# The logits' PSUM banks in one pool with the others, and an issue order written for it, in an attention and token-MLP block

## The chip, the core and the metric

The kernel runs on one core of a Trainium2 chip. The metric is the device time of one execution in microseconds (us); what is compared is the median of several executions.

## What is computed

One transformer block with conditioning, in bfloat16, for S = 2048 tokens of width D = 512:

```
sa, ca, ga, sb, cb, gb = (silu(c) @ w_mod) in six pieces
h = layernorm(x) * (1 + ca) + sa
# attention: 32 heads of 16, each query sees 8 keys, 2 positions apart, none before the start
x = x + ga * (local_attention(h @ wqkv) @ wo)
h = layernorm(x) * (1 + cb) + sb
# token MLP: mixes along S, F = 1792
u = gelu(einsum('bsd,sf->bdf', layernorm(h), w1) + b1)
x = x + gb * transpose(einsum('bdf,fs->bds', u, w2) + b2)
```

## The kernel before

The 2048 tokens are 16 tiles of 128. `SIZES = (2, 4, 4, 4, 2)` puts them into five chunks, and `build_chunk` (L634) records for each chunk the work of the attention: layer norm and its transposition, `qkv` products and their evacuations (`ev`), the products of query and key on DVE (`qk`), the sums over a head's 16 values as products with a 0/1 matrix on PE (`red`), which give the **logits**, then their maximum on DVE (`max`, L790), its subtraction by a product on PE (`sub`, L797), the exponential on ACT (`exp`, L800), the sum of the exponentials (`esum`), the softmax weights (`smB` on DVE). DMAs bring these weights into another layout (`a2`, four per chunk, into the tile `a2sb`) and the values too (`vd`, into a ring of five tiles `vD`); DVE multiplies the two (`pv`, four per chunk), PE sums (`pvacc`), ACT evacuates (`oev`). Then come the output projection (`wo`, one per token tile, L860), the residual sum (`x1`), the statistics of the second layer norm (`ln2q`, `rstd2`, `nb`, `n2`), its affine part on DVE (`aff`, two tiles per instruction, two passes), and the third layer norm (`ln3s` statistics, `rstd3`, `nb3`, `h3`). The token MLP's first product sums over tokens: `mlp1_{sweep}_{ft}_{tile}` (L927 on) adds the token tiles `h3`, as they get ready, for 14 blocks `ft` of 128 hidden values, and is parked in SBUF between sweeps (`park`, `padd`). `gelu`, the second product `mlp2_{tile}`, `fin` on DVE and the store `st_out` of each token tile end the kernel.

PSUM has eight banks of 512 float32 per partition. Six are single tiles `psS` (L313), a pool `ps` whose slots hold `qkv`, `esum`, `pvacc`, `wo` and MLP results; the other two are one tile `psL` (L314), which holds the logits of one chunk from the first `red` to `exp`. Chunks 1 to 3 use both of its banks, chunks 0 and 4 one.

The instruction order of every engine is written by hand in the string `ORDER` (L192 to 250). Each entry is an operation's name, with flags: `a`, `d`, `p` (ACT, DVE, POOL) or `s` (SP) choose the engine; on PE `q` splits each 128 x 128 product into four of 32 columns, one per column group of the array, and `n` leaves out a `wo`'s product that adds the residual (then `x1` adds it) or an `inj`. `fill:n` is n units of 128 columns of products that nobody reads. `schedule()` (L86) reads the string and gives each operation that needs a slot the free one that was freed longest ago. All engines issue through one wrapper, so every row of the profile has line L143; rows are told apart by their tiles. SP issues nearly all DMAs, in the string's order, and waits where one is not ready.

Of the kernel before, what the change touches and what calls it, by code (L numbers as in the profile page):

```python
# [8 lines left out]
ALU = mybir.AluOpType  # L9
# [4 lines left out]
P = 128  # L14
# [28 lines left out]
class _Graph:  # L43
# [42 lines left out]
    def schedule(self):  # L86
# [4 lines left out]
        for pos, token in enumerate(ORDER.split()):  # L91
# [22 lines left out]
            if o.alloc is not None:  # L114
                p = o.alloc.pool
                o.alloc.i = min((freed[p][k], k) for k in range(self.pools[p]) if held[p][k] is None)[1]
                held[p][o.alloc.i] = o.alloc
            if o.frees is not None:
                o.frees.left -= 1
                if o.frees.left == 0:  # L120
                    held[o.frees.pool][o.frees.i] = None
                    freed[o.frees.pool][o.frees.i] = pos
# [85 lines left out]
qk2_0 woq_s smB1 qk2_3 qkv2_01:q qkv2_12:q qkv2_02:q ev2_11:a ev2_01:a a2_1_1:a ev2_12:a ev2_02:a qk2_1 qk2_2 wo1:q  # L208
x1_1:a wo0:q x1_0:a ln2q1 xt10 xt12 red2_0 qkv2_23:q qkv3_22:q qkv3_12:q vd1_0 st_row1 vd1_2 ev2_23:a ln2q0 rstd2_0
nb1_4 nb2_0 qkv2_21:q ev2_21:a red2_1 a2_1_2:s a2_1_0:s a2_1_3:s vd1_1 ld_row1 vd1_3 n1_14:p pv1_2 qkv3_13:q red2_2  # L210
red2_3 max2 qkv2_22:q n1_15:a ev3_13:a n2_1:a ev3_12:a ev2_22:a n2_0:a halo_v2:p qkv2_20:q sub2:q ev2_20:a exp2
pvacc1_2 qkv3_10:q halo_v3:a oev1_2:a ev3_10:a qkv3_02:q qkv3_20:q pv1_1 qkv3_01:q pvacc1_1 esum2:q ev3_02:a ev3_20:a
ev3_22:a aff0 pv1_0 qkv3_03:q qkv3_00:q pvacc1_0 pv1_3 oev1_1:a ev3_01:a rcp2 halo_k3:a smB2 ln3s0 qkv3_11:q oev1_0:a
pvacc1_3 ev3_11:a oev1_3:a qkv3_23:q fill:1:q wo5:q wo3:q qk3_2 qk3_1 ld_w1_0_0 ld_w1_0_512 vd2_3 xt14 vd2_2 vd2_1
a2_2_1:s a2_2_0:s a2_2_2:s vd2_0 a2_2_3:s wo4:q ln3s1 ev3_03:a ev3_00:a qk3_0 x1_3:a x1_4:a qk3_3 ln2q3 ln2q4 x1_5:a
ev3_23:a qkv4_22:q qkv3_21:q ev3_21:a wo2:q red3_0 x1_2:a qkv4_20:q fill:2:q red3_1 qkv4_00:q red3_2 ev4_22:a ln2q5
ln2q2 ev4_20:a rstd2_2 pv2_0 rstd2_4 red3_3 pvacc2_0 oev2_0:a pv2_3 qkv4_12:q ev4_12:a qkv4_02:q nb2_2 ev4_02:a n2_2:a
max3 sub3:q pvacc2_3 exp3 esum3:q oev2_3:a rstd3_0 pv2_2 nb2_4 pvacc2_2 qkv4_10:q rcp3 n2_5:a oev2_2:a n2_4:a pv2_1
pvacc2_1 fill:4:q oev2_1:a wo6:q wo7:q wo8:q wo9:q ev4_00:a smB3 n2_3:p vd3_3 ld_w1_0_896 vd3_1 vd3_0 a2_3_2:s a2_3_3:s
a2_3_0:s a2_3_1:s vd3_2 ld_w2_1 aff2 nb3_0 aff4 h3_1:p h3_0:p halo_v4:p ln3s3:a ln3s2:d ln3s4:d ln3v3 ln3v2 ln3v4  # L220
ln3s5:a ln3v5 pv3_1 x1_8:a x1_7:a x1_6:a rstd3_2 ev4_10:a h3_3 h3_2 mlp1_0_1_0 mlp1_0_2_0 mlp1_0_5_0:q mlp1_0_3_0:q
pvacc3_1 rstd3_4 nb3_4 x1_9:a pv3_2 pv3_3 pv3_0 h3_4:a h3_5:a oev3_1:a mlp1_0_2_2:q mlp1_0_1_2:q mlp1_0_0_0:q
mlp1_0_0_2:q mlp1_0_3_2:q mlp1_0_0_4:q mlp1_0_5_2:q mlp1_0_5_4:q mlp1_0_3_4:q mlp1_0_1_4:q pvacc3_2 mlp1_0_2_4:q ln2q9
ln2q6 park0_0:a park0_1:a ln2q7 park0_2:a oev3_2:a qk4_0 qk4_2 mlp1_0_4_0:q mlp1_0_4_2:q pvacc3_3 mlp1_0_6_0:q ln2q8
oev3_3:a mlp1_0_6_2:q pvacc3_0 mlp1_0_6_4:q mlp1_0_4_4:q oev3_0:a mlp1_0_7_0:q wo13:qn red4_0 rstd2_6 nb2_6 park0_3:a
qk4_1 x1_13:d n2_9:a n2_6:a park0_4:a wo12:q n2_8:p ld_w1_0_1152 ld_w1_0_1408 vd4_1 ld_w2_3 vd4_2 vd4_0 vd4_3 n2_7:d
# [15 lines left out]
padd2_1 gelu1 gelu4 mlp1_2_3_11 mlp1_2_3_14 mlp1_2_2_14 mlp1_2_6_11 padd2_3 padd2_2 gelu2 padd2_6 gelu6 gelu3
mlp1_1_12_10 mlp1_2_5_11 mlp1_2_5_14 mlp1_1_11_10 padd2_5 padd1_11 gelu5 gelu9 padd1_12 mlp1_1_13_10 gelu12 gelu11
mlp2_0_0 padd1_13 gelu13 ld_w2_4 ld_w2_2 ld_w2_5 mlp2_0_0b ld_w2_7 ld_w2_9 ld_w2_11 ld_w2_13 mlp2_2_0 mlp2_6_0
mlp2_0_0c mlp2_3_0 mlp2_8_0 mlp2_4_0 fin0_0 st_out0_0 fin4_0 fin2_0 st_out2_0 fin6_0 st_out4_0 fpre gsc mlp2_9_0 fin3_0
fin8_0 st_out8_0 st_out6_0 mlp2_5_0 mlp2_1_0 fin1_0 mlp2_14_0 mlp2_10_0 st_out1_0 st_out3_0 fin5_0 ld_w2_15 fin10_0
# [7 lines left out]
def kernel(  # L254
# [34 lines left out]
    G = _Graph(dict(ps=6, big=NBIG, vd=NVD))  # L289
# [344 lines left out]
    def build_chunk(ch):  # L634
# [125 lines left out]

        for dlo in range(4):
# [316 lines left out]
```

## Time and profile before

| what | us |
|---|---|
| three runs | 198.40, 198.61, 198.69 (median 198.61) |
| the profiled execution | 198.75 |
| its span, from the first instruction to the last | 197.03 |
| busy in it: PE, DVE, ACT, POOL | 185.8, 157.3, 127.1, 22.8 |
| mean granted TensorE clock | 0.997 |

Rows of the timeline begin with the start and the length in us, then the engine, the line, the operation, what it writes <- what it reads, its shape, and how many instructions the row holds; behind it in brackets is the idle time before it and what ended that. 128\*128 and 128\*32 stand for the part of the array that a product uses. A product's end is modelled, so rows of PE overlap a little, and starts are the better guide.

### The profile page before, as it was taken

What the parts mean: (1) busy time and instruction counts of PE and PEld (TensorE: products, weight loads), DVE (VectorE), ACT (ScalarE), POOL (GpSimd) and SP (SyncE); (2) the same over time, 40 slices, a digit from 0 to 9 for tenths busy, and PEclk for the clock granted to TensorE, in tenths of its full rate; (3) what the DMA queues carried; (4) which work ended last, traced back from release to release, by engine and by line L of the source; (5) the groups of instructions that cost most, each with busy time, mean ns of one, the idle gap of its engine ahead of it and who ended that gap; (6) DMA issues with size and microseconds to landing.
All of it is one profiled execution on the core that took longest, in us unless ns stands there. A gap on an engine that the chain in (4) does not pass through costs nothing.

```text
span 197.0 us, 5568 instructions
## 1 busy us (share of the span) xinstructions
PE 185.8 (94%) x2331; PEld 99.5 (50%) x2343; DVE 157.3 (80%) x222; ACT 127.1 (64%) x304; POOL 22.8 (12%) x46
## 2 busy tenths in 40 slices
PE   3999999999999996899999999999999999999993
PEld 1476656565465674435554454444444444444462
DVE  2789999999999999999999999977550207864693
ACT  4799999898999999999997899735660000000000
POOL 4184003000500001130031000500000000000000
PEclk9999999999999999999999999999999999999998
DMA  5999695888997449180497494588999200144113
GB/s 156 357 355 341 226 259 137 101 201 253 302 303 268 149 144 322 34 218 14 136 245 208 91 255 97 157 273 177 290 348 339 61 0 15 38 130 99 53 53 107
DMA packets 53893, 36.02 MB, mean 183 GB/s; under 512 B 24428, under 2 KB 50668, under 8 KB 53868
## 3 DMA queue, kind: packets, MB, share of 16 engines
q1 hardware_dynamic: 52772, 35.27, 64.2%
q10 hardware_dynamic: 1096, 0.39, 0.8%
q8 instruction: 18, 0.29, 0.6%
q14 instruction: 7, 0.06, 0.1%
HBM read 22.55 MB, written 2.10 MB: 125 GB/s over the span
## 4 chain that ended last, share of the span: by engine, by line
PE 63%; DVE 21%; issue 5%; DMA 4%; SPq 3%; ACT 2%; DVEq 0%; ACTq 0%
PE psS L143 61%; DVE big L143 14%; DMA xx<-in_A_x_dram 4%; DVE h L143 4%; SPq L143 3%; PE psL L143 2%; DVE lsb L143 1%; DVE st L143 1%; ACT xx L143 1%; ACT junk L143 1%; DVE m L143 1%; DVE nb L143 0%; ACT k_f L143 0%; DVE woq L143 0%; ACT rs L143 0%
## 5 line engine op out<-in xcount | busy, mean ns | idle before, releaser
L143 PEld LDWEIGHTS <-wst 128*128 128x128 bf16 (+1 forms) x578 | 35.6, 101 | 32.7 <-issue 2.8
L143 PE MATMUL psS<-h,wst 128*32 128x512 bf16 (+1 forms) x350 | 50.1, 379 | 0.4 <-issue 0.2
L143 DVE TENSOR_TENSOR big<-a2sb,vD 128x4096 bf16<-128x4096 bf16 (+1 forms) x20 | 36.4, 1857 | 0.1
L143 DVE TENSOR_TENSOR big<-q_sb,k_f 128x4096 bf16<-128x4096 bf16 (+1 forms) x20 | 36.3, 1857 | 0.0
L143 PE MATMUL psS<-hT,w_qkv 128*32 128x512 bf16 (+1 forms) x576 | 29.0, 344 | 0.0
L143 DVE SCALAR_TENSOR_TENSOR h<-psS,bcol,rows_bc 128x512 f32<-128x512 f32 (+2 forms) x17 | 12.1, 709 | 21.2 <-PE psS L143 21.0
L143 PEld LDWEIGHTS <-w_qkv 128*32 128x32 bf16 (+1 forms) x618 | 21.2, 107 | 13.9
L143 PE MATMUL psS<-gT,big 128*128 128x512 bf16 x111 | 24.8, 379 | 0.1
L143 POOL TENSOR_SCALAR h<-xx,rs,nb 128x512 bf16<-128x512 bf16 x11 | 11.5, 1047 | 94.3 <-DVE nb L143 40.6
L143 PEld LDWEIGHTS <-big 128*128 128x128 bf16 x144 | 12.1, 98 | 13.8 <-DMA big<-in_w_mod_dram 0.5
L143 PE MATMUL psS<-woq,o_sb 128*32 128x512 bf16 (+1 forms) x220 | 16.7, 379 | 0.3 <-ACT o_sb L143 0.3
L143 ACT ACTIVATE gT<-psS,bcol 128x512 bf16<-128x512 f32 x14 | 8.9, 685 | 8.6 <-DVE psS L143 8.6
L143 DVE TENSOR_TENSOR psS<-psS,gT 128x512 f32<-128x512 f32 x14 | 9.4, 697 | 5.5 <-PE psS L143 5.5
L143 DVE TENSOR_TENSOR h<-h,xx 128x512 bf16<-128x512 f32 (+2 forms) x17 | 11.1, 652 | 2.6 <-DMA out_dram<-h 2.1
L143 PE MATMUL psS<-hT,wst 128*32 128x512 bf16 (+2 forms) x134 | 11.8, 355 | 0.2
L143 DVE TENSOR_TENSOR h<-h,rows_bc 128x1024 bf16<-128x1024 bf16 (+2 forms) x16 | 11.5, 718 | 0.5
L143 ACT ACTIVATE v_sb<-psS,qvb 128x512 bf16<-128x512 f32 (+1 forms) x20 | 11.1, 599 | 0.7 <-PE psS L143 0.7
L143 DVE BATCH_NORM_STATS2 st<-xx 128x6 f32<-128x512 bf16 x12 | 7.9, 681 | 4.5 <-DMA xx<-in_A_x_dram 4.5
L143 PEld LDWEIGHTS <-group 128*32 128x32 bf16 x288 | 7.7, 96 | 7.3 <-DVE big L143 1.7
L143 PE MATMUL psS<-big,group 128*32 128x512 bf16 (+1 forms) x160 | 9.9, 338 | 1.1 <-DVE big L143 0.8
L143 ACT ACTIVATE q_sb<-psS,qvb 128x512 bf16<-128x512 f32 (+1 forms) x18 | 10.6, 614 | 0.4 <-PE psS L143 0.3
L143 PEld LDWEIGHTS <-o_sb 128*32 128x32 bf16 (+1 forms) x220 | 7.0, 97 | 7.1 <-ACT o_sb L143 0.8
(106 smaller groups left out, 249.3 us busy)
## 6 DMA issues: line engine op xcount, KB each, us to landing
vD<-v_sb SPq DMA_DIRECT2D x12, 524.5 KB, 5.1
big<-in_B_w_dram SPq DMA_DIRECT2D x4, 896.0 KB, 8.3
vD<-v_sb SPq DMA_DIRECT2D x8, 268.5 KB, 2.5
wst<-in_B_w_dram SPq DMA_DIRECT2D x3, 640.0 KB, 4.4
out_dram<-h SPq DMA_DIRECT2D x15, 128.0 KB, 1.8
wst<-in_B_w_dram SPq DMA_DIRECT2D x2, 800.0 KB, 5.4
xx<-in_A_x_dram SPq DMA_DIRECT2D x6, 256.0 KB, 7.2
gT<-in_w_mod_dram SPq DMA_DIRECT2D x4, 384.0 KB, 7.6
```

The costliest lines, as they stand in the source:

```text
L143: r = fn(*a, **k)
```

## The change

The six single banks and the logits' double bank become four double tiles `psT`, and the pool `ps` has eight slots, two in each tile. The logits of a chunk now ask the pool for a slot: for chunks 1 to 3 an aligned pair of banks, for chunks 0 and 4 one bank, taken by the first `red` and given back by `exp`. `schedule()` hands out pairs. From the 237th entry on, where before the first output projections stand, the string `ORDER` is rewritten: entries move, and some change their engine or flags. The entries ahead of it are the same.

```
-                o.alloc.i = min((freed[p][k], k) for k in range(self.pools[p]) if held[p][k] is None)[1]
-                held[p][o.alloc.i] = o.alloc
+                z = o.alloc.size
+                o.alloc.i = min((max(freed[p][k:k + z]), k) for k in range(0, self.pools[p] - z + 1, z)
+                                if held[p][k:k + z] == [None] * z)[1]
+                held[p][o.alloc.i:o.alloc.i + z] = [o.alloc] * z
...
-    G = _Graph(dict(ps=6, big=NBIG, vd=NVD))
+    G = _Graph(dict(ps=8, big=NBIG, vd=NVD))
...
-    psS = [psp.tile([P, 512], F32, name=f"psS{i}") for i in range(6)]
-    psL = psp.tile([P, 2, 512], F32, name="psL")
+    psT = [psp.tile([P, 2, 512], F32, name=f"psT{i}") for i in range(4)]
...
-        return psS[slot.i][:]
+        return psT[slot.i // 2][:, slot.i % 2, :]
...
+        s_L = _Slot("ps", NW // WPM)
+
+        def lps(hf, s_L=s_L):
+            return psT[(s_L.i + hf) // 2][:, (s_L.i + hf) % 2, :]
...
-            add("pe", 0.02 + NW // WPM * _t_mm(WPM * SB), f, reads=["consts", "big_use"], frees=s_, writes=["psL"],
-                name=f"red{ch}_{dlo}", tiled=True)
+            add("pe", 0.02 + NW // WPM * _t_mm(WPM * SB), f, reads=["consts", "big_use"], frees=s_,
+                name=f"red{ch}_{dlo}", tiled=True,
+                **(dict(alloc=s_L) if dlo == 0 else dict(writes=[s_L])))
```

Of the string, two lines from the end of the attention and the last lines show how the entries moved (`wo11:q` becomes `wo11:qn`, some `mlp1` lose or get `q`, stores come in another order):

```
-qk4_3 wo11:q red4_1 red4_2 red4_3 ln2q13 x1_12:a ln2q12 park0_5:a x1_11:a rstd2_12 aff6 ln3s7:a mlp1_0_9_0 mlp1_0_9_2
+wo11:qn wo10:qn ld_w1_0_1152 ld_w2_2 ld_w1_0_1408 vd4_1 vd4_0 vd4_3 vd4_2 aff6 ln3s7:a max4 mlp1_0_9_0 sub4 exp4
...
-mlp2_7_0 mlp2_12_0 mlp2_11_0 fin7_0 st_out10_0 st_out7_0 fin12_0 st_out5_0 fin9_0 st_out9_0 fin11_0 fin14_0 st_out11_0
-mlp2_13_0 fin13_0 st_out13_0 st_out12_0 st_out14_0 mlp2_15_0 fin15_0 st_out15_0 mlp2_15_1 fin15_1 st_out15_1 mlp2_15_2
+fin11_0 st_out8_0 st_out10_0 st_out5_0 fin9_0 mlp2_13_0 fin14_0 ld_w2_15 st_out11_0 st_out9_0 fin13_0 st_out13_0
+st_out14_0 mlp2_12_0 fin12_0 st_out12_0 mlp2_15_0 fin15_0 st_out15_0 mlp2_15_1 fin15_1 st_out15_1 mlp2_15_2 fin15_2
```

`wo10` had its `n` before (`wo10:n`) and now also `q`; that of `wo11` is new.

Three places of the order in rows. First, DVE at the end of chunk 2, before (`lsb` is the softmax weights of chunk 3, `h_104` the second layer norm's output, `rows_bc` its affine rows, `st`, `mv` and `nb` the third layer norm's statistics; the row with `nb` is `nb3_0`, which POOL's `h3_0` and `h3_1` need):

```order
L143 TENSOR_TENSOR lsb_89<-lsb_89,rb 128x1024
L143 TENSOR_TENSOR h_104<-h_104,rows_bc 128x1024 x2
L143 SCALAR_TENSOR_TENSOR nb_140<-mv_137,rs_139 128x2
L143 TENSOR_TENSOR h_104<-h_104,rows_bc 128x1024 x2
L143 BN_STATS st_2_136<-h_104 128x6 x2
```

The same place after:

```order
L146 TENSOR_TENSOR lsb_86<-lsb_86,rb 128x1024
L146 TENSOR_TENSOR h_101<-h_101,rows_bc 128x1024 x4
L146 BN_STATS st_2_133<-h_101 128x6
L146 SCALAR_TENSOR_TENSOR nb_137<-mv_134,rs_136 128x2
L146 BN_AGGR mv_134<-st_2_133 128x2
```

`nb3_0` has moved behind the second `aff` and one statistic. Second, SP in chunk 1, before (`hT` is the layer norm transposed, whose two rows are `xt10` and `xt12`; `a2sb` the softmax weights' DMAs `a2_1_2`, `a2_1_0`, `a2_1_3`; `vD` the values):

```order
L143 DMA_TRANSPOSE hT_78<-h_76 128x8x128 x2
L143 DMA vD_101<-v_sb_83 128x1x2098
L143 DMA scratch<-mrows 4x3x128
L143 DMA vD_99<-v_sb_83 128x1x2098
L143 DMA a2sb_91<-lsb_89 128x2x128 x3
L143 DMA vD_97<-v_sb_83 128x1x2098
```

And after:

```order
L146 DMA_TRANSPOSE hT_75<-h_73 128x8x128
L146 DMA scratch<-mrows 4x3x128
L146 DMA vD_94<-v_sb_80 128x1x2098
L146 DMA rows_bc<-scratch 128x1536
L146 DMA a2sb_88<-lsb_86 128x2x128
L146 DMA_TRANSPOSE hT_75<-h_73 128x8x128
L146 DMA a2sb_88<-lsb_86 128x2x128
```

The second transpose has moved between two of the weights' DMAs, of which the third is on ACT's queue now. Third, PE in the first sweep of the token MLP (`h_76`, after `h_73`, holds the token tiles, `wst` the weights; 32x512 is a split product, 128x512 a full one). Before, its third entry, `mlp1_0_5_0`, begins so:

```order
L143 MATMUL psS_67<-h_76,wst_105 128x512
L143 LDWEIGHTS wst_105
L143 MATMUL psS_67<-h_76,wst_105 128x512
L143 LDWEIGHTS wst_106
L143 MATMUL psS_63<-h_76,wst_106 32x512
L143 LDWEIGHTS wst_106
L143 MATMUL psS_63<-h_76,wst_106 32x512
```

After, from the end of the sixth entry, `mlp1_0_0_0`, through `mlp1_0_0_2` to `mlp1_0_1_2`:

```order
L146 MATMUL psT_65<-h_73,wst_102 32x512
L146 LDWEIGHTS wst_102
L146 MATMUL psT_65<-h_73,wst_102 128x512
L146 LDWEIGHTS wst_102
L146 MATMUL psT_65<-h_73,wst_102 128x512
L146 LDWEIGHTS wst_102
L146 MATMUL psT_66<-h_73,wst_102 128x512
```

Before, the MLP's products are split from the third entry on until chunk 4's logits; now full ones stand between split ones.

More of the change, by code (lines that the diff above doesn't have):

```diff
@@ L120, in schedule @@
                 if o.frees.left == 0:
-                    held[o.frees.pool][o.frees.i] = None
-                    freed[o.frees.pool][o.frees.i] = pos
+                    z, k = o.frees.size, o.frees.i
+                    held[o.frees.pool][k:k + z] = [None] * z
+                    freed[o.frees.pool][k:k + z] = [pos] * z
             done.add(o.idx)
@@ L207 @@
 fill:6:q qkv2_13:q esum1:q pvacc0_3 n1_12:a n1_13:a ev2_13:a ev2_03:a oev0_2:a pvacc0_0 pvacc0_1 rcp1 rstd1_4 oev0_0:a
[L208 to L226, printed above, removed]
@@ L242 @@
[L242 to L246, printed above, removed]
@@ L247 @@
-mlp2_7_0 mlp2_12_0 mlp2_11_0 fin7_0 st_out10_0 st_out7_0 fin12_0 st_out5_0 fin9_0 st_out9_0 fin11_0 fin14_0 st_out11_0
-mlp2_13_0 fin13_0 st_out13_0 st_out12_0 st_out14_0 mlp2_15_0 fin15_0 st_out15_0 mlp2_15_1 fin15_1 st_out15_1 mlp2_15_2
-fin15_2 st_out15_2
+qk2_0 woq_s smB1 qk2_3 qkv2_01:q qkv2_12:q qkv2_02:q ev2_11:a ev2_01:a a2_1_1:a ev2_12:a ev2_02:a qk2_1 qk2_2 vd1_2
+vd1_3 xt10 st_row1 vd1_0 ld_row1 a2_1_0:s xt12 a2_1_3:s vd1_1 a2_1_2:a wo1:q wo0:q red2_0 qkv2_20:q qkv2_23:q qkv2_21:q
+red2_1 qkv2_22:q x1_0:a x1_1:a nb1_4 ln2q0 ev2_20:a ln2q1 rstd2_0 qkv3_00:q red2_2 red2_3 qkv3_10:q pv1_0 nb2_0 n2_1:p
@@ new lines @@
+max2 ev2_21:a n1_15:a n1_14:a ev2_22:a n2_0:a halo_v2:a ev3_10:a halo_k3:a ev3_00:a ev2_23:a pvacc1_0 qkv3_01:q
+ev3_01:a pv1_1 aff0 pv1_3 pv1_2 qkv3_11:q fill:8:q sub2:q exp2 fill:1:q qkv3_13:q pvacc1_1 fill:4:q esum2:q xt14
+qkv4_02:q qkv3_02:q oev1_1:a ev3_13:a oev1_0:a ln3s0 ev3_11:a rcp2 ln3s1 smB2 ld_w1_0_0 vd2_1 vd2_3 vd2_0 ld_w1_0_512
+a2_2_0:s a2_2_3:s a2_2_2:s a2_2_1:s vd2_2 qk3_0 qk3_1 qkv3_21:q pvacc1_3 qkv3_22:q pvacc1_2 qkv3_12:q qkv3_03:q
+ev3_02:a oev1_2:a oev1_3:a ev3_22:a ev3_12:a ev3_03:a wo3:q x1_3:a halo_v3:a qkv3_20 ev3_20:a wo4:q ln2q3 wo2:q qk3_3
@@ new lines @@
+x1_4:a ln2q4 x1_2:a ln2q2 wo5:q x1_5:a rstd3_0 ev3_21:a red3_0 red3_1 qkv4_20:q pv2_3 pvacc2_3 qkv4_10:q qkv3_23 qk3_2
+red3_2 rstd2_2 ev4_20:a ln2q5 ev3_23:a ev4_02:a nb2_2 red3_3 qkv4_12:q pv2_0 max3 sub3:q qkv4_00:q qkv4_22:q pvacc2_0
+rstd2_4 n2_2:a nb2_4 n2_5:a exp3 ev4_12:a pv2_2 pv2_1 esum3:q pvacc2_2 oev2_3:a oev2_0:a rcp3 oev2_2:a n2_4:a pvacc2_1
+oev2_1:a wo8:q wo6:q wo7:q wo9:q smB3 n2_3:p halo_v4:p vd3_3 vd3_2 vd3_0 vd3_1 a2_3_2:s a2_3_0:s a2_3_1:s a2_3_3:s
+ev4_22:a ld_w1_0_896 ld_w2_1 aff2 ln3s3:a aff4 ln3s2:d nb3_0 ln3v2 ln3v3 ln3s5:d ev4_10:a rstd3_2 x1_6:a ln3s4:d ln3v5
@@ new lines @@
+ln3v4 h3_0:p h3_1:p h3_3 h3_2 rstd3_4 x1_7:a nb3_4 pv3_3 pv3_2 pv3_0 pv3_1 h3_5:a x1_9:a x1_8:a ln2q6 h3_4:a ln2q7
+ev4_00:a ln2q9 mlp1_0_3_0:q mlp1_0_2_0:q mlp1_0_3_2:q mlp1_0_1_0:q mlp1_0_4_0:q mlp1_0_0_0:q mlp1_0_0_2 mlp1_0_1_2
+mlp1_0_4_2 mlp1_0_6_0:q mlp1_0_1_4:q mlp1_0_0_4:q mlp1_0_2_2:q park0_0:a ln2q8 park0_1:a rstd2_6 mlp1_0_5_0:q
+mlp1_0_3_4:q mlp1_0_5_2:q mlp1_0_4_4:q pvacc3_2 oev3_2:a nb2_6 pvacc3_0 mlp1_0_2_4:q park0_2:a pvacc3_3 mlp1_0_6_2:q
+oev3_0:a pvacc3_1 mlp1_0_5_4:q n2_7:a oev3_1:a oev3_3:a mlp1_0_6_4 mlp1_0_7_0 mlp1_0_7_2 n2_8:a n2_6:a n2_9:a park0_3:a
@@ new lines @@
+park0_4:a qk4_1 qk4_2 qk4_0 qk4_3 wo13:qn wo12:q x1_12:a ln2q12 park0_5:a mlp1_0_7_4:q red4_0 red4_1 red4_2 red4_3
+wo11:qn wo10:qn ld_w1_0_1152 ld_w2_2 ld_w1_0_1408 vd4_1 vd4_0 vd4_3 vd4_2 aff6 ln3s7:a max4 mlp1_0_9_0 sub4 exp4
+ln3s8:d x1_13:d ln3s9:d ln3v8 esum4 ln3s6:d ln3v9 ln3v7 ln3v6 ln2q13 park0_6:a rcp4 rstd2_12 rstd3_6 smB4 a2_4_2:a
+a2_4_1:s nb2_12 nb3_6 h3_9:d x1_11:d x1_10:d n2_13:a h3_8:a a2_4_3:s a2_4_0:s n2_12:d aff12 h3_7:p h3_6:p mlp1_0_9_2
+mlp1_0_8_0 mlp1_0_8_2 mlp1_0_12_0 mlp1_0_12_2 mlp1_0_10_0 mlp1_0_10_2 mlp1_0_8_4:q mlp1_0_9_4:q mlp1_0_12_4:q
@@ new lines @@
+mlp1_2_3_14 mlp1_2_2_14 mlp1_2_0_11 ld_w1_1_1408 ld_w1_2_640 ld_w2_3 ld_w2_0 mlp1_2_0_14 padd2_2 gelu8 gelu9 padd2_3
+gelu2 mlp1_2_1_11 mlp1_2_6_11 gelu3 gelu10 padd2_0 padd2_4 gelu0 gelu7 gelu4 mlp1_1_12_10 mlp1_2_1_14 padd2_1 padd2_6
+gelu1 gelu6 mlp1_2_5_11 mlp1_2_5_14 mlp1_1_13_10 padd2_5 gelu5 mlp1_1_11_10 fpre padd1_13 padd1_12 padd1_11 gelu13
+gelu12 gelu11 gsc mlp2_0_0 ld_w2_5 mlp2_5_0 mlp2_1_0 mlp2_2_0 mlp2_0_0b mlp2_0_0c ld_w2_4 ld_w2_7 fin2_0 fin1_0 fin0_0
+ld_w2_9 ld_w2_13 st_out1_0 st_out0_0 mlp2_8_0 mlp2_4_0 fin4_0 st_out2_0 st_out4_0 fin8_0 fin5_0 ld_w2_11 mlp2_3_0
@@ L250 @@
+mlp2_6_0 mlp2_7_0 fin3_0 st_out3_0 mlp2_10_0 fin6_0 st_out6_0 fin10_0 fin7_0 mlp2_14_0 mlp2_11_0 mlp2_9_0 st_out7_0
+fin11_0 st_out8_0 st_out10_0 st_out5_0 fin9_0 mlp2_13_0 fin14_0 ld_w2_15 st_out11_0 st_out9_0 fin13_0 st_out13_0
+st_out14_0 mlp2_12_0 fin12_0 st_out12_0 mlp2_15_0 fin15_0 st_out15_0 mlp2_15_1 fin15_1 st_out15_1 mlp2_15_2 fin15_2
+st_out15_2
 """
@@ L548, in fill_fn @@
         for r in [4] * (n // 4) + [1] * (n % 4):
-            mm(psS[k][:, 0:r * P], lhsT=ident[:], rhs=ident[:].unsqueeze(1).to_broadcast([P, r, P]), start=True, stop=True)
+            mm(psT[k // 2][:, k % 2, 0:r * P], lhsT=ident[:], rhs=ident[:].unsqueeze(1).to_broadcast([P, r, P]), start=True, stop=True)
     G.fill_fn = fill_fn
```

43 lines of the change are left out of this document (20 added, 23 removed).

## The prediction

> **What bounds the kernel now.** I read the busy shares by slice first, then the same shares by stretch, then the chain of work that ended last. In the page, PE's row is full from the second slice on and sags once, near slices 16 to 18; DVE's row is full up to there and thins afterwards.
>
> ```profile
> PE   3999999999999996899999999999999999999993
> DVE  2789999999999999999999999977550207864693
> PE 63%; DVE 21%; issue 5%; DMA 4%; SPq 3%; ACT 2%; DVEq 0%; ACTq 0%
> ```
>
> By stretch (columns: us, then the busy time of PE, PEld, DVE, ACT and POOL with instruction counts, clock, DMA share, GB/s):
>
> ```profile
> 43.00:71.50 28.50, 28.29 (x605) 17.11 (x601) 28.46 (x19) 27.30 (x65) 2.94 (x2) 1.00 0.83 238
> 71.50:86.10 14.60, 11.65 (x280) 6.71 (x271) 14.40 (x19) 13.97 (x37) 3.21 (x4) 1.00 0.63 199
> 86.10:88.70 2.60, 2.26 (x27) 0.78 (x28) 2.60 (x3) 2.57 (x10) 0.00 (x0) 1.00 1.09 237
> 88.70:190.50 101.80, 101.22 (x688) 47.66 (x697) 71.63 (x119) 45.91 (x107) 5.53 (x6) 1.00 0.55 149
> 190.50:197.03 6.53, 3.12 (x43) 2.80 (x40) 3.18 (x7) 0.00 (x0) 0.00 (x0) 0.92 0.26 80
> ```
>
> Up to 71.5 PE and DVE are both full. From 71.5 to 86.1 DVE stays full (14.40 of 14.60) and PE loses 2.95. From 88.7 to 190.5 PE is full (101.22 of 101.80). So the time is three pieces, which is also what the chain says (PE 63%, DVE 21%): DVE's chain up to about 82.6, which decides when PE gets chunk 2's last input; PE's plain sum of work from there; and the way out after PE's last product. Who held PE near 80 is in its groups of waits (total us, times, longest):
>
> ```profile
> PE psL L143 <- DVE m L143: 1.3, 2, 1.0
> PE psS L143 <- DVE big L143: 0.8, 2, 0.7
> PE psS L143 <- ACT lsb L143: 0.8, 1, 0.8
> ```
>
> These are the softmax and `pv` steps of chunk 3 and 2, data that DVE and ACT make. None is a wait for a free bank. The first 236 entries of the order are the same in both kernels, so nothing changes before roughly 43 us.
>
> **The change, part by part.** Times are against the profiled execution: 198.75, of which the span is 197.03 and 1.7 lies outside. It is 0.14 above the median of the three runs (198.61).
>
> *DVE's chain to `pv2_1`.* DVE has no gap here, so what counts is the sum of what stands ahead of `pv2_1`, not its order.
>
> ```profile
> 49.79 2.28 DVE L143 TENSOR_TENSOR big<-a2sb,vD 128x4096 bf16<-128x4096 bf16 x1
> 61.65 8.89 DVE L143 TENSOR_TENSOR big<-q_sb,k_f 128x4096 bf16<-128x4096 bf16 x4
> 70.46 4.48 DVE L143 TENSOR_TENSOR big<-a2sb,vD 128x4096 bf16<-128x4096 bf16 x2
> 78.34 2.28 DVE L143 TENSOR_TENSOR big<-a2sb,vD 128x4096 bf16<-128x4096 bf16 x1
> 80.54 0.68 DVE L143 TENSOR_TENSOR lsb<-lsb,rb 128x1024 bf16<-128x1024 bf16 x1
> ```
>
> The new order puts one `pv2` inside the four `qk3`, moves `max2`, `max3` and two `aff` passes, and has the same instructions ahead of `pv2_1`. So `pv2_1` again ends at 80.6 and PE starts `wo8`/`wo9` as before, which end near 86.1. What joining the banks and six more fill units do earlier is swallowed by that wait: **0**. Without that cover the six units of 128 columns would cost a quarter of 0.216 each (a 512-column product, below), 0.33.
>
> *Start of the token MLP.* These are the rows of PE, then DVE, POOL and ACT there.
>
> ```profile
> 82.86 1.04 PE L143 MATMUL psS<-woq,o_sb 128*32 128x512 bf16 x16
> 83.94 1.04 PE L143 MATMUL psS<-woq,o_sb 128*32 128x512 bf16 x16
> 85.88 0.39 PE L143 MATMUL psS<-xx,ident 128*32 128x512 bf16 x4
> 86.20 2.17 PE L143 MATMUL psS<-h,wst 128*128 128x512 bf16 x19
> 88.67 0.61 PE L143 MATMUL psS<-big,group 128*32 128x512 bf16 x8 [0.29 <-ACT k_f L143]
> 81.14 1.41 DVE L143 TENSOR_TENSOR h<-h,rows_bc 128x1024 bf16<-128x1024 bf16 x2
> 82.47 0.15 DVE L143 SCALAR_TENSOR_TENSOR nb<-mv,rs 128x2 f32<-128x2 f32 x1
> 82.54 1.87 DVE L143 TENSOR_TENSOR h<-h,rows_bc 128x1024 bf16<-128x1024 bf16 x2
> 84.33 1.27 DVE L143 BATCH_NORM_STATS2 st<-h 128x6 f32<-128x512 bf16 x2
> 75.18 0.77 POOL L143 TENSOR_SCALAR h<-xx,rs,nb 128x512 bf16<-128x512 bf16 x1 [22.28 <-PE psS L143]
> 82.80 2.25 POOL L143 TENSOR_SCALAR h<-h,rs,nb 128x512 bf16<-128x512 bf16 x2 [6.85 <-ACT q_sb L143]
> 86.45 0.59 ACT L143 ACTIVATE xx<-psS 128x512 bf16<-128x512 f32 x1
> 88.03 0.58 ACT L143 ACTIVATE k_f<-psS 128x512 bf16<-128x512 f32 x1
> ```
>
> Two `wo` blocks of five sets each start 1.08 apart (82.86, 83.94), so a set of four 32-column products, like a full one, is 0.216. Before, PE ran eight MLP products between 86.20 and 88.67. They are 8 x 0.216 = 1.73 of work, so 0.74 of the 2.47 was lost: the products took banks that ACT was still emptying (`x1_7` ends 87.04, `ev4_10` 88.61), and the tiling mode changed once. In effect PE started at 88.67 - 1.73 = 86.94. This is the one place where a bank is waited for, and with eight banks I take that as gone. What is late next is POOL: `nb3_0` now stands behind `aff4` and `ln3s2` instead of ahead of them. The four `aff` passes then run without POOL beside them: 81.14 + 2 x 1.33 (the step from 81.14 to 82.47) = 83.8; plus one statistic, 0.6, plus `nb3_0`, 0.15: 84.6; two POOL passes at the undisturbed 0.77: 86.15; with 0.2 to the first product, 86.35 to 86.45, just after `wo9`. Gain 86.94 - 86.4 = **-0.5**. Bounds: if POOL again takes 2.25 for its pair, 86.85 + 0.2 = 87.05 and the term is +0.1; if nothing is late, PE goes on at 86.15 and it is -0.8. I take the undisturbed 0.77, since the DVE work beside it is now statistics, not the passes it fell beside.
>
> *`wo11` with its residual product left out.* It removes one set, 0.216; DVE, 71.63 of 101.80 busy there, adds instead: **-0.22**. `x1_11` thereby goes to DVE; with DVE full it would cost some 0.69, as the addition in the row at 191.35 below.
>
> *Changes of tiling mode.* In the second half, sets of four 32-column products (128*32) and full ones (128*128) alternate: between the first MLP product and the end, three changes before (the one near 87 is inside the 0.74 above) and nine after. The price stands in rows like these:
>
> ```profile
> 101.51 0.83 PE L143 MATMUL psL<-big,group 128*32 128x512 bf16 x12
> 102.28 1.25 PE L143 MATMUL psS<-h,wst 128*128 128x512 bf16 x4
> ```
>
> Three sets from 101.51 are done at 102.16, the next starts at 102.28: 0.12. From `wo9`'s last set, 85.88, to 86.20 it is 0.32 - 0.216 = 0.10. I take 0.105: 6 x 0.105 = **+0.63**. PE is full there, so all of it counts. The four further changes that are new lie before 82, in PE's waiting time, and cost nothing; without that cover, 0.42. Bounds by these rows: 6 x 0.10 to 6 x 0.12, 0.6 to 0.72.
>
> The Trainium skill has a rule on this, in TensorEngine Tiling (Array Packing), Key Properties: a change of the tiling mode, not merely of the tile, drains TensorE. That speaks against the change, and the two rows agree that something is paid. TensorE: Matmul & The Clock Gate, in Step-by-step: what each phase is for, gives the drain as about 128 cycles, 53 ns at its 2.4 GHz; by that figure (an estimate from that page) the term would be +0.32 in place of +0.63 and the sum 0.31 lower.
>
> *The last stores.* SP and DVE at the end:
>
> ```profile
> 192.07 2.75 SPq L143 DMA_DIRECT2D out_dram<-h  x6
> 191.35 0.69 DVE L143 TENSOR_TENSOR h<-h,xx 128x512 bf16<-128x512 f32 x1
> 193.65 0.29 DVE L143 TENSOR_TENSOR h<-psS,fpre 128x128 bf16<-128x128 f32 x1
> ```
>
> Before, six stores (tiles 13, 12, 14 and the three parts of 15) queue on SP from 192.07 to 194.82, 0.46 each, because tile 13, which is finished last of the full ones, stands ahead of 12 and 14. The last piece is ready at 193.94 and issued 0.42 late. After, 13 and 14 go as they are finished, and only 12 and the three parts are left: the last issue can begin near 193.97 and ends at 194.45: **-0.35** (0 if the stores of 13 and 14 bunch up too).
>
> *New waits.* In the new order the pieces of softmax weights that `pv` reads (`a2`) are issued differently: `a2_1_3` goes behind the DMA transpose `xt12` on SP, and the first `pv2` comes 2.2 earlier, at 61.65 + 3 x 2.2 = 68.25 instead of 70.46.
>
> ```profile
> 39.22 2.05 SPq L143 DMA_TRANSPOSE hT<-h  x1
> 43.49 2.91 SPq L143 DMA_DIRECT2D a2sb<-lsb  x3
> 61.76 1.99 SPq L143 DMA_DIRECT2D a2sb<-lsb  x3
> 64.45 1.69 SPq L143 DMA_DIRECT2D a2sb<-lsb  x1
> DMA to landing us min/median/max: 2.0/3.4/4.2
> ```
>
> First place: 43.49 + 0.64 for `a2_1_0`, + 2.05 for the transpose: `a2_1_3` is issued at 46.2 and lands between 48.2 and 50.4, for a `pv1_0` that DVE reaches at 49.79: -1.6 to +0.6 of lateness. Second: four issues from 61.76, 0.65 each, the last at 63.7 (65.4 with one as long as the 1.69), landing at 65.7 to 69.6 for 68.25. DVE has no slack, so any lateness moves all that follows. Bounds for both: 0 to 0.6 and 0 to 1.35. With the median landing both are in time; I take **+0.1**, and keep +1.9 as the far end.
>
> Sum: -0.5 - 0.22 + 0.63 - 0.35 + 0.1 = -0.34. Against the profiled 198.75 this is 198.4; against the median, **198.3**.
>
> **The rivals.**
>
> *The time is made up of the late `a2` pieces (slower).* For: DVE has been full since before 43, and both moves take away margin. Against: median landings are in time. It decides from a landing of 3.6 us on `a2_1_3` or a last `a2_2` issue after 64.9. Price 0.6 to 1.9 on top of a sum of -0.44: typically +1.2, so 198.61 + 0.8 = 199.4.
>
> *The switches are paid and the start is not gained.* POOL takes 2.25 again: the first term is +0.1 instead of -0.5, the rest as above, so +0.26: 198.9, the same within what can be told.
>
> *The banks matter where I say they don't.* If the sag of 71.5 to 86.1 were a matter of banks, PE could win up to 2.95 and the time would be 195.7. For: the waits near 80 are on the logits' tile. Against: their releasers are DVE's `m` and `big` and ACT's `lsb`, and DVE is full until `pv2_1`.
>
> *A change of mode costs less than I take.* Both rows of its price are starts after a long run of products of the other kind; if part of the 0.10 to 0.12 is a late weight load, runs placed otherwise can hide it. With half of it hidden the term is +0.32 and the time 198.0. The drain alone, by the page named above, would come out at that too. Against: in both rows PE waited for nothing that the profile names, and the two agree within 0.02.
>
> *The change does not do what it says.* It says that two banks more are free for others. If nobody takes them when they would be waited for, the 0.74 at 87 stays: that is the second rival's time, and I hold them together.
>
> **How the numbers follow.** Forecast as summed, 198.3 with its own range 197.9 to 198.6: 0.48, of which 0.24 lies below 198.21 and 0.24 above. Late pieces, 199.4: 0.30. Start not gained, 198.9: 0.10, of which 0.03 is above 199.0. Cheap switches, 198.0: 0.07. Banks matter, 195.7: 0.05. A measurement of this kernel can tell about 0.2% (0.4 us) from no change. So faster, below 198.21: 0.24 + 0.07 + 0.05 = 0.36; within: 0.24 + 0.07 = 0.31; slower, above 199.01: 0.30 + 0.03 = 0.33. The range leaves out the large gain, part of the cheap switches and the far end of the late pieces: 197.7 to 199.9.
>
> **What would show it.** In the profile after: `pv2_1` ends at 80.6 on DVE; POOL's two passes at 0.77 each and the first MLP product near 86.4, with no bank wait behind it; nine gaps of about 0.1 where 128*32 and 128*128 meet after 87; SP's last row of stores with four, not six; no DVE idle time released by `a2sb`. Idle time of DVE before 71 with a DMA as releaser would make the prediction wrong, and so would PE filling 71.5 to 86.1 while DVE's chain ends early.

## The result, and the profile after

The changed kernel takes **244.4 us** (median of 4 runs, 243.7 to 244.88) against 198.65 beside it for the kernel before (198.4 to 198.8): ratio 1.230, 95% interval 1.227 to 1.232. The forecast was 198.3. Nothing of this size stood among the rivals.

The page of the kernel after, its busy times, its slices and its chain:

```profile
PE 196.7 (81%) x2326; PEld 102.8 (42%) x2339; DVE 158.0 (65%) x222; ACT 128.9 (53%) x302; POOL 21.1 (9%) x45
PE   2778679859859988768867199976897999999983
DVE  3724969988792888999457792293834606654382
PEclk9979999999979999997999859999999999999999
PE 61%; ACT 23%; DVE 8%; issue 3%; DMA 3%; SPq 1%; ACTq 0%; DVEq 0%
```

Before, PE's row was full from the second slice on, with one sag; now it sags everywhere, from the start. The work is the same (DVE 158.0 after 157.3, ACT 128.9 after 127.1), but ACT has gone from 2% to 23% of the chain: PE and ACT take turns. PE is idle for 242.8 - 196.7 = 46.1, against 197.0 - 185.8 = 11.2 before.

Whom PE waited for (total us, times, longest), in the kernel after:

```profile
PE psT L146 <- DVE xx L146: 6.6, 2, 5.1
PE psT L146 <- ACT v_sb L146: 4.9, 4, 2.0
PE psT L146 <- ACT o_sb L146: 4.7, 3, 2.5
PE psT L146 <- ACT gT L146: 4.1, 4, 1.5
PE psT L146 <- ACT xx L146: 3.9, 2, 2.7
```

All five releasers are instructions that *read* PSUM: the evacuations of `qkv` (`v_sb`), `oev` (`o_sb`), `park` (`gT`) and the sums `x1` (`xx`). Before, the waits near 80 us were for data (`m`, `big`, `lsb`); these are for banks: all but one of them (0.97 for `o_sb`, ahead of a `wo` product) stand ahead of products that do not read the tile named.

The most telling place is early, where both kernels have the same order and the same banks. PE transposes tile 0 into bank 2, ACT copies it out in four instructions (`hT`; the row of before holds two more), and PE runs fill products into bank 3, whose results nobody reads. ACT and PE before:

```profile
10.47 2.71 ACT L143 ACTIVATE hT<-psS,a1col 128x256 bf16<-128x256 bf16 x6
9.09 1.24 PE L143 MATMUL psS<-ident 128*128 128x512 bf16 x5
```

And after:

```profile
10.24 1.19 ACT L146 ACTIVATE hT<-psT,a1col 128x256 bf16<-128x256 bf16 x3
13.56 0.47 ACT L146 ACTIVATE hT<-psT,a1col 128x256 bf16<-128x256 bf16 x1 [2.14 <-PE psT L146]
11.47 2.06 PE L146 MATMUL psT<-ident 128*128 128x512 bf16 x5 [1.61 <-ACT hT L146]
```

Now the fill into bank 3 waits until ACT's third copy out of bank 2 is done, and ACT's fourth copy, which stands behind the fill in the order, waits until the fill is done. Before, the fill waited for nothing: it was over (10.33) when ACT's copies began. (Five fill products take 2.06 after and 1.24 before; the granted clock between 10 and 15 us is 0.67 after and 1.00 before.) Neither touches the other's bank. These waits are in the program. The rows of the order show it, ACT and PE before:

```
L143 ACTIVATE hT_77<-psS_65,a1col 128x256 [waits DVE_49,PE_49]
L143 ACTIVATE hT_77<-psS_65,a1col 128x256 x3
...
L143 MATMUL psS_66<-ident 128x512
```

and after:

```
L146 ACTIVATE hT_74<-psT_64,a1col 128x256 [waits DVE_49,PE_49]
L146 ACTIVATE hT_74<-psT_64,a1col 128x256 x2
L146 ACTIVATE hT_74<-psT_64,a1col 128x256 [waits PE_49]
...
L146 MATMUL psT_64<-ident 128x512 [waits Activation_49]
```

`psS_65` and `psS_66` were two tiles; both are `psT_64` now, and the waits that the framework puts in here go by the tile. By the first attention product on DVE, still in the part of the order that was not touched, 7.15 us are lost: before, then after:

```profile
17.46 4.63 DVE L143 TENSOR_TENSOR big<-q_sb,k_f 128x2048 bf16<-128x2048 bf16 x4
```

```profile
24.61 4.63 DVE L146 TENSOR_TENSOR big<-q_sb,k_f 128x2048 bf16<-128x2048 bf16 x4
```

The longest wait shows the same at work in the new part. `mlp1_0_9_2` goes on adding in bank 2; `wo10` has bank 3, and DVE reads that late, as `x1_10`. PE after, then DVE after:

```profile
133.59 0.38 PE L146 MATMUL psT<-m,nident 128*128 128x512 bf16 x1
139.02 1.44 PE L146 MATMUL psT<-h,wst 128*128 128x512 bf16 x3 [5.05 <-DVE xx L146]
```

```profile
138.27 0.69 DVE L146 SCALAR_TENSOR_TENSOR xx<-psT,xx 128x512 bf16<-128x512 f32 x1
```

PE's row begins when DVE's read of the neighbouring bank ends (138.96), and the wait is 5.05 long.

### The profile page after: what moved, and what is told of

Same layout as the page of the kernel before. It is cut to its first block, busy times and chain, and to the rows that moved or that the text cites. A ratio compares the mean times of both kernels' runs of the same rounds, so it can differ in the third digit from the quotient of the medians.

```text
span 242.8 us, 5558 instructions
## 1 busy us (share of the span) xinstructions
PE 196.7 (81%) x2326; PEld 102.8 (42%) x2339; DVE 158.0 (65%) x222; ACT 128.9 (53%) x302; POOL 21.1 (9%) x45
## 4 chain that ended last, share of the span: by engine, by line
PE 61%; ACT 23%; DVE 8%; issue 3%; DMA 3%; SPq 1%; ACTq 0%; DVEq 0%
PE psT L146 61%; ACT junk L146 4%; ACT v_sb L146 3%; DMA xx<-in_A_x_dram 3%; ACT h L146 2%; DVE h L146 2%; ACT gT L146 2%; ACT k_f L146 2%; ACT xx L146 2%; DVE gT L146 1%; ACT o_sb L146 1%; ACT q_sb L146 1%; ACT w_qkv L146 1%; DVE xx L146 1%; DVE st L146 1%
## 5 line engine op out<-in xcount | busy, mean ns | idle before, releaser
L146 PE MATMUL psT<-h,wst 128*32 128x512 bf16 (+1 forms) x361 | 55.2, 411 | 15.6 <-DVE xx L146 6.6
L146 PE MATMUL psT<-hT,w_qkv 128*32 128x512 bf16 (+2 forms) x552 | 31.1, 355 | 5.8 <-ACT o_sb L146 2.5
L146 DVE SCALAR_TENSOR_TENSOR h<-psT,bcol,rows_bc 128x512 f32<-128x512 f32 (+2 forms) x17 | 12.1, 709 | 20.6 <-PE psT L146 20.4
L146 PE MATMUL psT<-gT,big 128*128 128x512 bf16 x110 | 24.9, 379 | 0.1
L146 PE MATMUL psT<-big,group 128*32 128x512 bf16 (+1 forms) x288 | 18.9, 356 | 7.1 <-ACT v_sb L146 2.5
L146 PE MATMUL psT<-woq,o_sb 128*32 128x512 bf16 (+1 forms) x232 | 16.4, 380 | 2.9 <-ACT gT L146 1.9
L146 ACT ACTIVATE v_sb<-psT,qvb 128x512 bf16<-128x512 f32 (+1 forms) x20 | 11.5, 601 | 4.6 <-PE psT L146 4.4
L146 PE MATMUL psT<-hT,wst 128*32 128x512 bf16 (+2 forms) x134 | 11.8, 355 | 1.9 <-ACT hT L146 0.8
L146 ACT ACTIVATE k_f<-psT 128x512 bf16<-128x512 f32 x16 | 9.5, 591 | 5.6 <-PE psT L146 5.6
L146 ACT ACTIVATE q_sb<-psT,qvb 128x512 bf16<-128x512 f32 (+1 forms) x18 | 10.7, 614 | 2.9 <-PE psT L146 2.8
```

The lines of the kernel that those rows point to most:

```text
L146: r = fn(*a, **k)
```

## The experiments

Theory T: accesses to the two halves of a double tile are made to wait for one another, and the layout alone costs the 46 us. Rival R: the rewritten order costs them.

**The old order on joined tiles.** Order, slots and bank addresses of before; only the declaration differs.

```
-    psS = [psp.tile([P, 512], F32, name=f"psS{i}") for i in range(6)]
+    psT = [psp.tile([P, 2, 512], F32, name=f"psT{i}") for i in range(3)]
...
-        return psS[slot.i][:]
+        return psT[slot.i // 2][:, slot.i % 2, :]
...
```

> The kernel before with its order, its slots and its banks unchanged; only the six single PSUM tiles are declared as the halves of three double tiles. Theory T (an access to one half of a double tile is made to wait for accesses to the other half, whatever the order): the time goes up by most of the 46 us, to 225 to 250. Rival R (the rewritten order is what costs, the joined tiles are harmless): 198.4 to 198.9, as before.

Measured: 255.65 against 198.84, ratio 1.286 (1.282 to 1.290). Rival R falls: without one entry of the order changed the loss is 57 us, more than that of the whole change. Since the banks are at the same places, it isn't the chip that makes two neighbouring banks wait, but the program's waits.

**The new order on tiles of their own.** Six single tiles again; the logits keep a double one; `schedule()` gives singles the double's halves only when nothing else is free.

```
-    psT = [psp.tile([P, 2, 512], F32, name=f"psT{i}") for i in range(4)]
+    psS = [psp.tile([P, 512], F32, name=f"psS{i}") for i in range(6)]
+    psL = psp.tile([P, 2, 512], F32, name="psL")
...
+                o.alloc.i = min((p == "ps" and (k < 6) == name.startswith("red"), max(freed[p][k:k + z]), k)
...
```

> The changed kernel's order, word for word, on a pool of eight banks in which six are tiles of their own and only the logits' two are one double tile (single slots go there only when no other is free, nine times). Theory T: nearly all of the 46 us is gone, and what is left is the worth of the new order, which the prediction put at -0.3: 197.7 to 200. Rival R: the order costs, so 235 to 245.

Measured: 210.15, ratio 1.060 (1.056 to 1.064). Most of the loss is gone, but neither theory had 11 us left over. PE's waits in this run:

```profile
PE psS L147 <- ACT gT L147: 2.5, 4, 1.0
PE psS L147 <- ACT o_sb L147: 2.5, 3, 1.3
PE psL L147 <- DVE xx L147: 1.9, 1, 1.9
```

The first are waits for banks again, on single tiles too. Of the second, two of the three (1.28 and 0.48) stand ahead of `wo` products, which read `o_sb`, so they can be for data. The third is of the joined kind, on the pair that is still one tile: PE writes one half of `psL` and waits for DVE's read of the other. Either an order written for eight banks is squeezed into six that come round sooner, or the order is bad in itself. That needed a run of its own, below.

**The old order on the changed kernel's pool.** The string of before in the kernel after, nothing else.

> The changed kernel with the order string of before put back: four double tiles, pool of eight slots, logits in it. Theory T: 225 to 250, near the kernel with joined tiles alone. Rival R: 198 to 199.

Measured: 238.14, ratio 1.198 (1.193 to 1.203). With four double tiles the old order loses 39 us, the new one 46: the new order is no remedy for the joined tiles, it suffers 6 us more (in another set of runs).

**One pair joined.**

```
+    psT = psp.tile([P, 2, 512], F32, name="psT")
+    psS = [psT[:, 0, :], psT[:, 1, :]] + [psp.tile([P, 512], F32, name=f"psS{i}")[:] for i in range(2, 6)]
...
```

> The kernel before with only the first two of its six single banks declared as one double tile. Theory T: the cost grows with the share of accesses that have a partner bank; a third of the singles is joined, so about a third of what the three joined pairs cost, 208 to 216. A rival to it, that one blocked pair is enough to hold the whole chain: 225 or more. Rival R: 198.4 to 198.9.

Measured: 220.22, ratio 1.108 (1.104 to 1.111), so +21.4. A miss by its number, since I had taken a third of 46; against the 57 of three pairs it is 38%. So three joined pairs cost more than one, and one pair alone doesn't cost as much as all. The number of pairs alone doesn't set the cost, though: the run before, with as many double tiles as the first one but eight slots to hand out in place of six (the logits' among them), lost 39 and not 57.

**New and old order, all eight banks tiles of their own.** With eight single tiles no instruction can span the logits' banks, so their maximum is two reductions and a maximum, and the exponential two instructions. The second run is the old order with six slots and the same split; the third the old order on the pool of eight.

```
+            for hf, m_ in zip(range(NW // WPM), (m1, m2_t[:, 0:SB])):
+                nc.vector.tensor_reduce(m_.unsqueeze(1), _ap(lps(hf)[:, 0:1], [[1, SB], [SB, WPM]]), mybir.AxisListType.X,
+                                        ALU.max)
+            if NW > WPM:
+                nc.vector.tensor_tensor(m1, m1, m2_t[:, 0:SB], op=ALU.max)
...
+            for hf in range(NW // WPM):
+                nc.scalar.activation(ee[:, hf * WPM:(hf + 1) * WPM, :].rearrange("p w s -> p (w s)"),
+                                     lps(hf)[:, 0:WPM * SB], ACT.Exp, scale=DH ** -0.5)
```

> The changed kernel's order and slots, but every one of the eight banks is a tile of its own; since no instruction can then span two, the maximum over a chunk's logits is two reductions and a maximum of the two, and the exponential two instructions. Theory T (the joined tiles are the whole loss, and the 11 us that the new order still lost with six tiles of its own came from reusing those six too soon): within 1 us of the run with the old order on eight tiles, 198 to 201. Rival O (the new order itself carries some 10 us of waits): 206 to 212.

> The kernel before with its logits' double tile as two single tiles and the same split of the maximum and the exponential: the price of the split alone. Both theories: 0.3 us of DVE for each of three chunks where DVE has no gap for two of them, 198.8 plus 0.3 to 1.2.

> The order of before on the pool of eight slots, all eight banks tiles of their own, maximum and exponential split: what the pool is worth alone, when nothing is joined. By the prediction's reading (banks are waited for only around 87 us, 0.6 at most): 0 to 0.6 below the run with the old order, six slots and the same split, so 199.0 to 199.6. If banks are what PE lacks from 71 to 86: 197 or less.

Measured: new order 199.93 (ratio 1.0055, 1.0031 to 1.0078); old order with six slots 199.57 (1.0039, 1.0020 to 1.0058); old order with eight slots 199.58, in another set of runs (1.0028, 1.0002 to 1.0054). So rival O falls as well: the 11 us belong to the layout of that run, six singles and a pair still joined. What share the sooner reuse of the six had in them, and what share the joined pair, was not measured. On independent banks the two orders can't be told apart (new over old 1.0055 / 1.0028 = 1.0027, give or take 0.0035 with the two half widths combined), and a pool of eight is worth nothing that shows to the old order. The split costs the old order 0.8.

**Sixteen more changes of tiling mode**, in the kernel before: the flag `q` taken from `mlp1_0_1_2`, `0_2`, `0_4`, `5_4`, `1_4`, `2_4`, `4_2` and `6_0`.

> The kernel before with eight of its split MLP products between 89 and 96 us given to the whole array instead, each between split ones: sixteen changes of tiling mode more on a PE that is full there. By the price of the prediction, 0.105 each: +1.7. By half of it, 0.053 each, which is the figure of the Trainium skill's page TensorE: Matmul & The Clock Gate (Step-by-step: what each phase is for) for a drain: +0.85.

Measured: 200.55 against 198.73, ratio 1.0077 (1.0049 to 1.0105), +1.8. In the trace, ten of the changes lie between the first `pvacc` of chunk 3 and the second. PE before, then in this run:

```profile
88.67 0.61 PE L143 MATMUL psS<-big,group 128*32 128x512 bf16 x8 [0.29 <-ACT k_f L143]
93.52 0.62 PE L143 MATMUL psS<-big,group 128*32 128x512 bf16 x8
```

```profile
90.03 0.62 PE L143 MATMUL psS<-big,group 128*32 128x512 bf16 x8 [0.29 <-ACT k_f L143]
95.98 0.62 PE L143 MATMUL psS<-big,group 128*32 128x512 bf16 x8
```

4.85 became 5.95: 0.11 a change, the price of the prediction. The whole, +1.0 to +2.1 by its interval, leaves out the 0.85 of half the price. The Trainium skill (TensorE: Matmul & The Clock Gate, Step-by-step: what each phase is for) has a last column need about 128 cycles to leave the array, 53 ns at 2.4 GHz as an estimate from that page; the price measured here is twice that.

**Stores in the order in which they are finished.**

```
-... fin12_0 st_out5_0 fin9_0 st_out9_0 fin11_0 fin14_0 st_out11_0
-mlp2_13_0 fin13_0 st_out13_0 st_out12_0 st_out14_0 ...
+... fin12_0 st_out5_0 st_out12_0 fin9_0 st_out9_0 fin11_0 fin14_0 st_out11_0
+st_out14_0 mlp2_13_0 fin13_0 st_out13_0 ...
```

> The kernel before with only the stores of token tiles 12, 13 and 14 issued in the order in which DVE finishes them. By the prediction's term: -0.35. If the last store is not what ends the span: 0.

Measured: 198.39 against 198.73, ratio 0.998 (0.9957 to 1.0003): the size that was expected, though the interval just reaches 1, so that the time alone doesn't show a gain. The trace is plainer. SP's last row in this run (from 192 on), then DVE's last:

```profile
191.81 2.44 SPq L143 DMA_DIRECT2D out_dram<-h  x4
```

```profile
193.39 0.29 DVE L143 TENSOR_TENSOR h<-psS,fpre 128x128 bf16<-128x128 f32 x1
```

There are four stores in place of six, and the last issue ends 194.25 - 193.68 = 0.57 after DVE's end, where before it was 194.82 - 193.94 = 0.88.

**Four small edits without the change.** Stores as above; `wo11:qn` with `x1_11:d`; `x1_6` and `x1_7` ahead of `ln3s5` on ACT, and `pv3_1` ahead of `ln3v5`; `mlp1_0_1_0` and `mlp1_0_2_0` split.

```
...
-ln3s5:a ln3v5 pv3_1 x1_8:a x1_7:a x1_6:a rstd3_2 ev4_10:a h3_3 h3_2 mlp1_0_1_0 mlp1_0_2_0 mlp1_0_5_0:q mlp1_0_3_0:q
+ln3s5:a pv3_1 ln3v5 x1_8:a rstd3_2 ev4_10:a h3_3 h3_2 mlp1_0_1_0:q mlp1_0_2_0:q mlp1_0_5_0:q mlp1_0_3_0:q
...
```

> The kernel before, on its own banks, with the gains that the prediction counted taken one by one without the change: stores of tiles 12 to 14 as finished (-0.35), the residual of tile 11 added on DVE (-0.22), the sums of tiles 6 and 7 on ACT moved ahead of the statistic of tile 5, so that their banks are free when the token MLP's first products want them (-0.3 to -0.5), and its first two products split as their neighbours are, two changes of tiling mode less (-0.21). If each term stands: -0.9 to -1.3, 197.4 to 197.9. If the order around the MLP's start was not what held PE: -0.35 to -0.6.

Measured: 199.01 against 199.08, ratio 0.9986 (0.9964 to 1.0008): in the middle a smaller gain than either expectation, though the interval, -0.7 to +0.2, doesn't exclude the smaller of the two. The trace names one loss. DVE, then PE, in this run:

```profile
101.62 0.69 DVE L143 SCALAR_TENSOR_TENSOR xx<-psS,xx 128x512 bf16<-128x512 f32 x1
104.63 0.68 DVE L143 TENSOR_REDUCE m<-psL 128x64 bf16<-128x512 f32 x1
```

```profile
105.37 0.38 PE L143 MATMUL psL<-m,nident 128*128 128x512 bf16 x1 [0.48 <-DVE m L143]
```

`x1_11` on DVE stands ahead of the maximum of chunk 4's logits, and PE waits 0.48 for that maximum, where before `sub4` followed without a wait. At this place the edit that was to give 0.22 cost more than it gave.

**Three of the edits**, the same without `wo11:qn`.

> The kernel before, on its own banks, with three of the four small edits of the run before last: stores as finished (-0.35), the sums of tiles 6 and 7 earlier on ACT and the MLP's first two products split (-0.6 from wo9 to the third group of MLP products, as that run's trace showed). The residual of tile 11 goes back to PE, because on DVE its 0.69 stood ahead of the maximum of chunk 4's logits and PE waited 0.64 for that. If that reading holds: -0.7 to -1.0, 197.7 to 198.1 where before is 198.7. If it doesn't: no better than the run with all four, -0.3.

Measured: **198.14** against 198.78, ratio 0.9961 (0.9946 to 0.9977), -0.64. The median lies just short of the -0.7 to -1.0 that was expected; the interval (-1.1 to -0.5) covers that range. This version is faster than both kernels. PE at the start of the MLP in this run:

```profile
85.82 0.39 PE L143 MATMUL psS<-xx,ident 128*32 128x512 bf16 x4
86.03 1.90 PE L143 MATMUL psS<-h,wst 128*32 128x512 bf16 x32
88.12 0.62 PE L143 MATMUL psS<-big,group 128*32 128x512 bf16 x8 [0.19 <-DVE big L143]
```

The MLP follows `wo9` without a gap (86.03 is 85.82 + 0.21), and from `wo9`'s last set to `pvacc` it is 2.30 where it was 88.67 - 85.88 = 2.79.

**The same with 25 more entries split**, to do without two changes of mode (`q` on 23 entries of the MLP from `mlp1_0_9_0` to `mlp1_0_11_6`, on `wo10` and on `sub4`).

> The same with the 25 full MLP products between chunk 4's logits and its sums, wo10 and sub4 also split in four, which takes away two changes of tiling mode in a stretch where PE is full. By 0.11 a change (the sixteen added changes cost 1.8): 0.2 below the run beside it. If splitting itself costs, through four times as many products to issue: above it.

Measured: 199.34, ratio 1.0029 (1.0014 to 1.0045), 1.2 above the run beside it. PE ran the split products as fast as full ones (50 sets of four in 10.98), but DVE met this:

```profile
113.46 1.22 DVE L143 TENSOR_TENSOR big<-a2sb,vD 128x2048 bf16<-128x2048 bf16 x1 [1.55 <-DMA a2sb<-lsb]
```

DVE waited for softmax weights here, although SP issued them at the same point (108.31, in the run beside it 107.99, with everything 0.3 later in this run). Why they landed late isn't settled; it was not tried further.

## Why the prediction was wrong

**The step that failed** is the first term, put at nothing: "What joining the banks and six more fill units do earlier is swallowed by that wait: **0**", together with "The first 236 entries of the order are the same in both kernels, so nothing changes before roughly 43 us". I treated the change of tiles as a renaming of the same eight banks and counted only slots. What decides a wait in this program is the tile, and the change leaves four PSUM tiles where there were seven. In the place of the 0 stand +57 us for joining the old kernel's three pairs, +39 for the pool of four double tiles with the old order, +46 with the new one. Seven of the 46 are there before DVE's first attention product, in the entries that are the same.

The rival on the other side, late `a2` pieces at +0.8, was the wrong mechanism. It exists (DVE waited 0.30 for one with the new order on eight tiles, and 1.55 in the last run), but in the changed kernel no wait of DVE names `a2sb`.

**The banks.** "None is a wait for a free bank" held for the kernel before: eight slots in place of six left the old order where it was (199.58 and 199.57). So the rival that banks fill the sag of 71 to 86 falls too. The prediction itself named one exception, the 0.74 lost near 87, and took it as gone with eight banks. The old order on the pool of eight, PE from `wo9`'s last set on:

```profile
86.60 0.39 PE L146 MATMUL psS<-xx,ident 128*32 128x512 bf16 x4
86.92 2.01 PE L146 MATMUL psS<-h,wst 128*128 128x512 bf16 x19
89.28 0.40 PE L146 MATMUL psS<-big,group 128*32 128x512 bf16 x4 [0.35 <-DVE big L146]
```

From `wo9`'s last set to `pvacc` it is 2.68 in place of 2.79: with the banks free, PE waits for DVE's `pv3_1` instead. Free banks alone were worth 0.1 there.

**The MLP's start**, forecast at -0.5. On eight tiles of their own the new order did as said. POOL, then PE, in that run:

```profile
86.84 1.52 POOL L146 TENSOR_SCALAR h<-h,rs,nb 128x512 bf16<-128x512 bf16 x2 [9.21 <-DVE mv L146]
```

```profile
88.01 0.39 PE L146 MATMUL psS<-xx,ident 128*32 128x512 bf16 x4
88.23 1.47 PE L146 MATMUL psS<-h,wst 128*32 128x512 bf16 x24
```

The pair takes 1.52 (2 x 0.77 forecast, 2.25 before) and the MLP follows `wo9` without a bank wait. That part of the mechanism was right; what it saved was not measured by itself. The old kernel got from 2.79 to 2.30 there with three edits at once: the two sums earlier on ACT, `pv3_1` earlier on DVE, and two products split, which takes away two changes of mode (0.2 by the price above).

**Changes of tiling mode**: 0.105 forecast, 0.11 measured. The rival that they cost half of it falls, and with it the prediction's sum from the Trainium skill's drain.

**The last stores**: -0.35 forecast, -0.34 measured, with an interval of -0.85 to +0.06; the traces show 0.31 at the end. **`wo11`**: PE has one set of 0.22 less to do, but I put DVE's side at nothing by DVE's mean load over 100 us (71.63 of 101.80), and at that place DVE was on PE's path. In the new order `x1_11` stands behind `max4`; whether it is free there was not measured by itself.

**The order as a whole**, forecast at -0.34 with 0.1 for new waits: 1.0027 of the old one on the same tiles, give or take 0.0035, that is between -0.2 and +1.2 us. The forecast's gain lies just outside that; whether the new order is as good as the old one or slightly worse stays open.

## What to carry to other kernels

Before counting what a new PSUM layout frees, ask what the waits are attached to: here one PSUM tile of two banks behaves as one buffer, so give two results that live at different times two tiles, and use a double tile only for one result that one instruction reads as a whole. A part of the program that "is the same" is the same only if its waits are too; comparing the waits of both programs row by row would have shown this before any time was predicted. And an engine's mean load over a long stretch says nothing of the place where an added instruction stands ahead of one that is waited for.

## What was not expected of the hardware

Neighbouring PSUM banks as such need no waiting for one another. In the kernel before, at the early place shown above, PE transposes tile 1 into bank 3 while ACT copies tile 0 out of bank 2 (from 10.47 on):

```profile
10.67 1.01 PE L143 MATMUL psS<-ident,h 128*128 128x128 bf16 x15 [0.28 <-DVE h L143]
```

The three runs with a tile for every bank take 199.57 to 199.93. This agrees with the Trainium skill, PSUM — Partial Sum Buffer, PSUM bank collisions raise a hardware error, which asks for guarding by bank and 32-partition quadrant.

PE lost more than the time that it stood idle. In the kernel after, its busy time went up by 10.9 (185.8 to 196.7) with nearly the same products, and the granted clock fell in several stretches (columns as in the prediction). How much of the 10.9 is the clock was not separated:

```profile
100.00:120.00 20.00, 15.33 (x229) 6.93 (x226) 16.78 (x23) 14.86 (x42) 1.52 (x2) 0.91 0.41 106
140.00:160.00 20.00, 18.28 (x136) 7.69 (x136) 10.45 (x19) 11.00 (x29) 0.77 (x1) 0.88 0.38 103
```

The run with four edits had the same on a small scale, in its profiled execution: after the waits near 76 to 78 the clock fell to little over half for some 3 us, in which the products took up to nearly twice their time (`esum3` to `pvacc2_1`).

```profile
76.00:78.00 2.00, 1.05 (x16) 0.45 (x16) 2.00 (x2) 2.00 (x4) 0.00 (x0) 1.00 1.01 395
78.00:80.00 2.00, 1.98 (x50) 1.46 (x52) 2.00 (x3) 1.84 (x6) 0.00 (x0) 0.55 0.12 46
80.00:82.00 2.00, 2.00 (x42) 1.55 (x36) 1.97 (x4) 1.49 (x3) 0.00 (x0) 0.59 0.03 8
```

The kernel before, in its profiled execution, has waits of the same length there (1.04 and 0.80) and kept a clock of 1.00, so the same idle time sometimes costs the clock and sometimes doesn't. Nothing ties it to the four edits: a mean clock of 0.991, as in this execution, stands in 4 of their 12 executions and in 7 of the 23 of the kernel before beside them. What decides it was not tried.
